# Laying out k by halves of its heads, reordering the first batch's denominators and splitting the last output tile

## The chip, the cores and the metric

One Trainium2 chip, of which the kernel uses one core. The figure compared is device microseconds (us) of one execution. The profile is a hardware recording of a single execution; its times are in us from the start of the span unless marked ns. In the text PE is TensorE (matrix products; PEld is its weight load), DVE is VectorE (elementwise), ACT is ScalarE (functions), POOL is GpSimd and SP is SyncE. The last two compute little here: POOL issues the transfers whose tables software writes, SP issues transfers through a hardware queue, and so does ACT at the start.

## The reference

```python
# q, k, v: 8 batches x 8 heads x 576 positions x 64, float32; pool = 8
k_p = k.reshape(B, H, Sp, pool, D).mean(axis=3)          # Sp = 72 pooled rows
v_p = v.reshape(B, H, Sp, pool, D).mean(axis=3)
scores = scale * np.matmul(q, k_p.transpose(0, 1, 3, 2))
scores = scores - np.max(scores, axis=-1, keepdims=True)
attn = np.exp(scores)
attn = attn / (np.sum(attn, axis=-1, keepdims=True) + 1e-09)
attn_out = np.matmul(attn, v_p)
x = attn_out.transpose(0, 2, 1, 3).reshape(B * S, H * D)  # 4608 tokens x 512
h = x @ w_in                                              # 512 -> 2048
g = 0.5 * h * (1.0 + np.tanh(c * (h + 0.044715 * h * h * h)))
out = g @ w_out                                           # 2048 -> 512, float32
```

## The kernel before

Attention runs batch by batch (8 of them), the two dense layers group by group: a group is 512 of the 4608 tokens, so there are 9 groups, g = 0 to 8. The attention output of a batch is written, transposed and in bfloat16, into `xT` (128 partitions = two heads x 64, four such pairs of heads, all tokens), which is what the first dense layer reads. The order of all instructions is written out by hand; each engine works through its own list in order.

**Loads.** Batch 0 comes in first: k and v by the SP and ACT queues, q by POOL (converted to bfloat16 on the way) in two halves of four heads. Then POOL loads the first dense weight `w_in` (two transfers), batch 1's k, q and v, the second dense weight `w_out` in four quarters, and q of batch 2. A k row is 8 positions x 64 = 512 floats, which are to be summed over the 8 positions. `load_k` (line 67) puts rows 0 to 511 of the 576 (8 heads x 72) on 128 partitions, four to a partition, and the 64 rows left over, all of them of head 7, in a fifth column on partitions 64 to 127. The same call loads v's pooled rows 64 to 71 of all heads (lines 74 to 76), 32 partitions for each four heads, into partitions 0 to 63 of that fifth column. `load_v` brings the other 64 rows per head.

**The first batch (lines 364 to 437).** DVE halves the 512 floats three times (`k_steps`: 512 to 256 to 128 to 64 sums, the last one written in bfloat16 to `kp`). PE transposes the result into a PSUM bank (`trans_k_mm`), and DVE copies it to `kT` twice, for each of the two halves of the columns of q (`trans_k_copy(b, e, ...)`, e = 0, 1). PE also transposes q (`trans_q`), copied out by ACT or DVE. `scores` multiplies and takes the exponential (ACT); `den0` sums the exponentials on PE against a tile of ones, `inverse0` takes logarithm and negative exponential on ACT, which gives 1/sum; `av0` multiplies by the pooled v, and `mult0` (DVE) scales the product into `xT`. c is the half of the tokens, pr the pair of heads. `spin` issues matmuls on a tile of zeros whose result nobody reads. After this come fills of constant regions for the later batches (lines 427 to 434) and the first eight matmuls of group 0.

**A group (lines 440 to 525).** First part: for each of 16 blocks of the 2048 hidden columns four matmuls of 128x512 (`p1_mm`, line 336), then the gelu on ACT (line 342). Beside it, DVE and PE prepare batch g + 1: `k_steps`, two small transfers that move v's last rows to their partitions (`v_moves`, SP queue), `v_steps`, and `trans_k` after block 9 (in group 0: q's transposes after blocks 12 to 15, `trans_k` after block 13 and `v_steps` at the end). Second part: for each of the four row tiles r of 128 tokens 16 matmuls (`p2_mm`, line 345) that accumulate in one bank, in which the score and value products of batch g + 1 are interleaved at fixed places (`pos`, line 501). In group 0 the first two row tiles advance together by quarters of `w_out` (line 516), so that the 9th, 17th and 25th matmuls are the first to read a new quarter. Groups 7 and 8 have no batch to interleave.

**Stores (lines 348 to 356).** When a row tile is complete, DVE copies it from PSUM to `osb` and four transfers of 32 tokens x 2 KB each go out on the SP queue; of the very last tile two go by ACT. The order of the tokens is such that each block of 32 columns of `xT` belongs to one (c, t): c is the half of the batch's tokens, t a block within it (0 to 8), and in the output a block's 32 rows are 18 rows apart. With `TP` = 9 blocks to a half,

```python
rows = out[b * S:(b + 1) * S].rearrange("(p t e) d -> e t p d", t=TP, e=2)
```

**Next loads.** In group g the loads for batch g + 2 are issued: q by POOL, then its transposition as one transfer on the SP queue (line 224), whose landing POOL waits for in `gate` (line 448), and then k and v by POOL.

Of the kernel before, what the change touches and what calls it, by code (L numbers as in the profile page):

```python
# [8 lines left out]
F32 = mybir.dt.float32  # L9
BF16 = mybir.dt.bfloat16  # L10
# [8 lines left out]
def kernel(  # L19
# [9 lines left out]
    nc = tc.nc  # L29
    B, H, S, D = q.shape  # L30
    Sp = S // 8
    N = B * S
    DM = H * D
# [9 lines left out]
    KR = 4  # L43
# [20 lines left out]

    kts = [consts.tile([128, KR + 1, 512], F32, name=f"kt{i}") for i in range(2)]

    def load_k(b, engs):
        rows = k[b].rearrange("h (j l) d -> (h j) (l d)", l=8)
        main = rows[0:128 * KR].rearrange("(p r) c -> p r c", r=KR)
        n = KR // len(engs)  # L70
        for i, eng in enumerate(engs):
            eng.dma_start(out=kts[b % 2][:, i * n:(i + 1) * n], in_=main[:, i * n:(i + 1) * n])
        engs[0].dma_start(out=kts[b % 2][64:128, KR], in_=rows[128 * KR:])
        rows = v[b].rearrange("h (j l) d -> j h (l d)", l=8)
        for i in range(2):
            engs[-1].dma_start(out=kts[b % 2][32 * i:32 * i + 32, KR], in_=rows[64:, 4 * i:4 * i + 4])

# [20 lines left out]
    load_k(0, [nc.sync, nc.scalar])  # L98
# [10 lines left out]
    load_k(1, [nc.gpsimd])  # L109
# [10 lines left out]
    kps = [consts.tile([128, KR + 2, D], BF16, name=f"kp{i}") for i in range(2)]  # L120
# [6 lines left out]
    nc.vector.memset(idle, 0.0)  # L127
    nc.vector.memset(kTs[0][0], 0.0)
# [9 lines left out]
    def add(o, a, b):  # L138
        nc.vector.tensor_tensor(out=o, in0=a, in1=b, op=ALU.add)  # L139

    def k_steps(b, c=slice(0, KR + 1)):


        t = kts[b % 2]
        return [lambda: add(t[:, c, 0:256], t[:, c, 0:256], t[:, c, 256:512]),
                lambda: add(t[:, c, 0:128], t[:, c, 0:128], t[:, c, 128:256]),
                lambda: add(kps[b % 2][:, c], t[:, c, 0:64], t[:, c, 64:128])]

    def v_moves(b):

        for i in range(2):
            nc.sync.dma_start(out=vps[b % 2][64 - 64 * i:72 - 64 * i, 4 * i:4 * i + 4, 0],
                              in_=kps[b % 2][32 * i:32 * i + 32, KR])
# [13 lines left out]
    def half_bank(bank):  # L167
        return PS[:, bank, :].bitcast(BF16)

    def trans_k_mm(b, bank, r0=0, r1=KR + 1, n=128):  # L170
        tp = half_bank(bank)[:, 0:(KR + 1) * 128].rearrange("p (r c) -> p r c", c=128)
        kf = kps[b % 2].rearrange("p r d -> p (r d)")
        for r in range(r0, r1):
            nc.tensor.transpose(out=tp[:n, r, :], in_=kf[:, r * D:r * D + n], identity=identb)  # L174

    def trans_k_copy(b, e, bank, lower=True, upper=True):


        tp = half_bank(bank)[0:D, 0:(KR + 1) * 128].rearrange("p (r c) -> p r c", c=128)
        o = kTs[b % 2][e][e * 64:(e + 1) * 64]  # L180
        copy = nc.vector.tensor_copy

        def heads(h0, h1, c0, j0, j1):
            copy(out=o[:, h0:h1, c0:c0 + (j1 - j0) * KR].rearrange("p h (j r) -> p h j r", r=KR),  # L184
                 in_=tp[:, 0:KR, h0 * KH:h1 * KH].rearrange("p r (h j) -> p h j r", j=KH)[:, :, j0:j1])

        if lower:
            heads(0, 4, 0, 0, KH)
        if upper:
            heads(4, H - 1, 64, 0, 16)  # L190
            heads(4, H - 1, 0, 16, KH)
            copy(out=o[:, H - 1, 64:72].rearrange("p (j r) -> p j r", r=KR),
                 in_=tp[:, 0:KR, (H - 1) * KH:128].rearrange("p r j -> p j r"))
            copy(out=o[:, H - 1, 72:128], in_=tp[:, KR, 64:120])
            copy(out=o[:, H - 1, 0:8], in_=tp[:, KR, 120:128])

    def trans_k(b, bank):
        trans_k_mm(b, bank)
        for e in range(2):
            trans_k_copy(b, e, bank)  # L200
# [17 lines left out]
    def trans_q(b, i, t0, n, bank, eng):  # L218
        trans_q_mm(b, i, t0, n, bank)
        trans_q_copy(b, i, t0, n, bank, eng)  # L220
# [107 lines left out]
    def o_bank(g, r):  # L328
        return 1 - x_bank(g) if r % 2 == 0 else x_bank(g)
# [14 lines left out]
    def p2_mm(g, r, fo):  # L344
        nc.tensor.matmul(out=PS[:, o_bank(g, r), :], lhsT=gTs[g][:, fo, r * 128:(r + 1) * 128], rhs=w_out_b[:, fo, :],  # L345
                         start=(fo == 0), stop=(fo == FO - 1))

    def store(g, r):
        osb = opool.tile([128, DM], F32, name="osb")
        nc.vector.tensor_copy(out=osb, in_=PS[:, o_bank(g, r), :])  # L350

        for n in range(4):
            b, c = divmod(g * GROUP + r * 128 + n * 32, S)
            rows = out[b * S:(b + 1) * S].rearrange("(p t e) d -> e t p d", t=TP, e=2)
            eng = nc.scalar if (g, r) == (NG - 1, 3) and n % 2 else nc.sync
            eng.dma_start(out=rows[c // CH, c % CH // 32], in_=osb[n * 32:(n + 1) * 32, :])


    def spin(n, bank):

        for _ in range(n):
            nc.tensor.matmul(out=PS[:, bank, :], lhsT=idle[:, 0:128], rhs=idle, start=True, stop=True)  # L362

    act_set(EXP_SET)
    spin(22, 1)
    for f in k_steps(0, slice(0, KR)):
        f()
# [5 lines left out]
    trans_k_mm(0, 4, 0, KR, D)  # L373
    trans_k_copy(0, 0, 4, upper=False)
    trans_q(0, *QG[0], 5, nc.scalar)
    trans_q(0, *QG[1], 6, nc.vector)
    trans_k_copy(0, 1, 4, upper=False)
# [3 lines left out]
    for f in k_steps(0, slice(KR, KR + 1)):  # L381
        f()
    scores(1, 0, 2)
    trans_k_mm(0, 4, KR, KR + 1, D)
    trans_k_copy(0, 0, 4, lower=False)

    for h in range(H):
        i = h // 4
        nc.tensor.matmul(out=PS[64 - 64 * i:72 - 64 * i, 7, h * D:(h + 1) * D],
                         lhsT=identb[0:64, 32 * i + h % 4:32 * i + 32:4], rhs=kps[0][0:64, KR],  # L390
                         start=True, stop=True)
# [9 lines left out]
    trans_k_copy(0, 1, 4, lower=False)  # L401
# [9 lines left out]
    spin(4, 4)  # L411
    av0(0, 0, 4)
    mult0(0, 0, 4)
    den0(0, 2, 2)
    inverse0(0, 2, 2)
    av0(1, 0, 0)
    mult0(1, 0, 0)
    spin(3, 6)
    den0(1, 2, 6)
    inverse0(1, 2, 6)  # L420
    spin(3, 4)
    av0(0, 2, 4)
    mult0(0, 2, 4)
    spin(3, 0)
    av0(1, 2, 0)
    mult0(1, 2, 0)
    for t in kps:
        nc.vector.memset(t[:, KR + 1], 0.0)
# [11 lines left out]
    for g in range(NG):  # L440
# [3 lines left out]
        def load_next():  # L444

            load_q(g + 2)
            trans_q_dma(g + 2)
            nc.gpsimd.tensor_copy(out=gate, in_=qTs[g + 2][0:1, 1, TP - 1, 0:2])  # L448
            load_k(g + 2, [nc.gpsimd])
            load_v(g + 2, [nc.gpsimd])  # L450
# [62 lines left out]
        seq = [(r, fo) for r in range(4) for fo in range(FO)]  # L513
# [3 lines left out]
        for m, (r, fo) in enumerate(seq):  # L517
            for f, a in todo.pop(m, []):
                f(*a)
            p2_mm(g, r, fo)  # L520
            if fo == FO - 1:
                store(g, r)
        for m in sorted(todo):
            for f, a in todo[m]:
                f(*a)

# [29 lines left out]
```

The softmax here doesn't subtract the row's maximum and nothing guards it: scores larger than these inputs give would overflow.

## Time and profile before

| what | value |
|---|---|
| runs | 309.18, 308.51, 309.1 us; median 309.1 |
| the profiled execution | 308.29 us, of which the recorded span is 306.5 |
| PE busy | 298.2 us (97%), 1518 matmuls |
| DVE, ACT, POOL busy | 150.4 (49%), 219.0 (71%), 36.3 (12%) |
| TensorE clock granted | 0.999 |
| first matmul of group 0 | 22.08 us |
| second part of group 0 begins | 37.18 us |
| last copy from PSUM (line 350) | 302.11, 0.69 us long |
| read from HBM, written to HBM | 36.70 MB, 9.44 MB |

"Busy" of PE is from modelled ends, so 97% says that PE nearly always has a matmul in hand, not that it runs at its peak. The chain of waits follows the work that ended last back to the start: its rows are a start, a length and what filled it, and a DMA in it is a transfer that something waited for. A row of the timeline is a start, a length, the engine, the line, the operation, and in brackets the idle time before it and what ended that.

### The profile page before, as it was taken

How to read it: one execution, taken by the hardware profiler on the slowest of the kernel's cores; microseconds unless marked ns; L12 is line 12 of the kernel's file. 1: busy time of each engine (PE TensorE's matmuls, PEld its weight loads, DVE VectorE, ACT ScalarE, POOL GpSimd, SP SyncE). 2: the span in 40 equal slices, each digit the busy share in tenths (PEclk: the TensorE clock that was granted, in tenths of full speed). 3: DMA queues.
4: the chain of work that ended last, by engine and by line, in shares of the span. 5: the costliest groups of instructions: out<-in, count | busy, mean ns of one | idle time of the engine just before them, and what ended most of it. 6: DMA issues, size and time to landing. Idle time of an engine off the chain costs nothing.

```text
span 306.5 us, 4325 instructions
## 1 busy us (share of the span) xinstructions
PE 298.2 (97%) x1518; PEld 157.4 (51%) x1548; DVE 150.4 (49%) x334; ACT 219.0 (71%) x402; POOL 36.3 (12%) x69
## 2 busy tenths in 40 slices
PE   8999999999999999999999999999999999999994
PEld 3555555555555555555555555555555555445441
DVE  5868557573677057806681559245933630110021
ACT  1686679868987798779977998789868987206400
POOL 7103002305004000220014000400000000000000
PEclk9999999999999999999999999999999999999999
DMA  7999996987957952596159725662101210121022
GB/s 225 266 257 253 214 186 137 299 176 177 269 146 167 247 122 51 114 282 156 34 112 266 168 56 106 200 151 71 35 1 36 63 41 2 34 70 34 2 70 68
DMA packets 30359, 41.12 MB, mean 134 GB/s; under 512 B 18113, under 2 KB 18113, under 8 KB 29441
## 3 DMA queue, kind: packets, MB, share of 16 engines
q0 software_dynamic: 7856, 25.43, 34.9%
q1 hardware_dynamic: 21888, 14.09, 19.2%
q10 hardware_dynamic: 592, 1.31, 1.2%
q8 instruction: 12, 0.20, 0.3%
q14 instruction: 11, 0.08, 0.1%
HBM read 36.70 MB, written 9.44 MB: 151 GB/s over the span
## 4 chain that ended last, share of the span: by engine, by line
PE 83%; DMA 12%; POOL 1%; issue 1%; ACT 0%; DVE 0%; POOLq 0%
PE PS L345 38%; PE PS L336 36%; DMA kt<-in_k_dram 7%; DMA w_out_b<-in_moe_w_out_dram 5%; PE PS L239 4%; PE PS L261 4%; PE PS L174 1%; POOL w_in_b L105 0%; POOL qb L86 0%; POOL w_out_b L113 0%; DVE osb L350 0%; ACT e L247 0%; ACT ld L269 0%; ACT ld L268 0%; POOL identb masks.py:199 0%
## 5 line engine op out<-in xcount | busy, mean ns | idle before, releaser
L345 PE MATMUL PS<-w_out_b,gT 128*128 128x512 bf16 x560 | 134.2, 379 | 0.9
L336 PE MATMUL PS<-xT,w_in_b 128*128 128x512 bf16 x563 | 126.2, 379 | 0.6
L342 ACT ACTIVATE gT<-PS 128x512 bf16<-128x512 f32 x144 | 81.1, 604 | 47.5 <-PE PS L336 47.4
L336 PEld LDWEIGHTS <-w_in_b 128*128 128x128 bf16 x576 | 64.7, 113 | 57.2
L345 PEld LDWEIGHTS <-gT 128*128 128x128 bf16 x576 | 56.1, 97 | 56.7 <-issue 1.1
L350 DVE COPY osb<-PS 128x512 f32<-128x512 f32 x36 | 24.9, 691 | 98.3 <-PE PS L345 95.3
L279 DVE TENSOR_TENSOR xT<-PS,rc 64x288 bf16<-64x288 f32 x112 | 51.0, 455 | 31.6 <-ACT rc L271 29.3
L247 ACT ACTIVATE e<-PS 72x576 bf16<-72x576 f32 (+1 forms) x64 | 41.0, 646 | 9.1 <-PE PS L239 8.2
L239 PE MATMUL PS<-qT,kT 128*72 128x288 bf16 (+1 forms) x128 | 25.9, 286 | 0.9 <-ACT qT L214 0.6
L271 ACT ACTIVATE rc<-ld 128x288 f32<-128x288 f32 x56 | 24.8, 443 | 1.8
L314 ACT ACT_TABLE_LOAD x17 | 21.8, 1283 | 4.3 <-issue 4.1
L268 ACT ACTIVATE ld<-PS 64x288 f32<-64x288 f32 x56 | 22.8, 407 | 1.3
L269 ACT ACTIVATE ld<-PS 64x288 f32<-64x288 f32 x56 | 22.5, 402 | 1.3
L261 PE MATMUL PS<-e,vp 72*128 72x288 bf16 (+1 forms) x112 | 23.1, 286 | 0.0
L139 DVE TENSOR_TENSOR kt<-kt 128x1280 f32<-128x1280 f32 (+5 forms) x18 | 18.8, 1044 | 5.5 <-DMA kt<-in_v_dram 2.6
L239 PEld LDWEIGHTS <-kT 128*72 128x72 bf16 (+1 forms) x128 | 13.2, 105 | 15.2 <-DVE qT L216 1.2
L448 POOL COPY gate<-qT 1x2 bf16<-1x2 bf16 x6 | 1.0, 174 | 140.0 <-DMA qT<-qb 140.0
L139 DVE TENSOR_TENSOR vt<-vt 128x1024 f32<-128x1024 f32 (+1 forms) x16 | 15.3, 956 | 1.8 <-DMA vt<-in_v_dram 1.5
L184 DVE COPY kT<-PS 64x288 bf16<-64x288 bf16 (+2 forms) x48 | 13.0, 319 | 6.2 <-PE PS L174 6.1
L362 PE MATMUL PS<-idle 128*128 128x512 bf16 x39 | 11.9, 447 | 1.2 <-DVE idle L127 1.2
L261 PEld LDWEIGHTS <-vp 72*128 72x128 bf16 (+1 forms) x112 | 11.0, 98 | 3.8
L81 POOL DMA_DIRECT2D vt<-in_v_dram x14 | 9.0, 655 | 7.5 <-DMA w_in_b<-in_moe_w_in_dram 5.5
(47 smaller groups left out, 90.0 us busy)
## 6 DMA issues: line engine op xcount, KB each, us to landing
out_dram<-osb SPq DMA_DIRECT2D x142, 64.0 KB
kt<-in_k_dram POOLq DMA_DIRECT2D x7, 1024.0 KB, 6.2
vt<-in_v_dram POOLq DMA_DIRECT2D x14, 512.0 KB, 8.6
qb<-in_q_dram POOLq DMA_DIRECT2D x7, 576.0 KB, 11.6
w_in_b<-in_moe_w_in_dram POOLq DMA_DIRECT2D x2, 1024.0 KB, 16.7
w_out_b<-in_moe_w_out_dram POOLq DMA_DIRECT2D x4, 512.0 KB, 13.9
kt<-in_k_dram POOLq DMA_DIRECT2D x7, 128.0 KB, 5.9
kt<-in_v_dram POOLq DMA_DIRECT2D x14, 64.0 KB, 5.7
```

The costliest lines, as they stand in the source:

```text
L139: nc.vector.tensor_tensor(out=o, in0=a, in1=b, op=ALU.add)
L239: nc.tensor.matmul(out=PS[:n, bank + e, :CH].rearrange("j (t p) -> j t p", p=32), lhsT=kTs[b % 2][c][:, h, :n], rhs=qTs[b][:, h // 4, :, h ...
L247: nc.scalar.activation(out=e[:n], in_=PS[:n, bank:bank + 2, :CH], func=ACT.Exp, scale=1.0 / 64.0)
L261: nc.tensor.matmul(out=PS[:, bank + x, :CH], lhsT=window(vps[b % 2][:n], 2 * pr + x), rhs=e[:n, x, :], start=True, stop=True)
L268: nc.scalar.activation(out=ld[0:64], in_=PS[64:128, bank, :CH], func=ACT.Ln)
L269: nc.scalar.activation(out=ld[64:128], in_=PS[0:64, bank + 1, :CH], func=ACT.Ln)
L271: nc.scalar.activation(out=rc, in_=ld, func=ACT.Exp, scale=-1.0)
L279: nc.vector.tensor_tensor(out=xT[rows, pr, col:col + CH], in0=PS[rows, bank + x, :CH], in1=rc[rows], op=ALU.mult)
L336: nc.tensor.matmul(out=PS[:, h_bank(g, fo), c0:c1], lhsT=w_in_b[fo // 8][:, ko, q * 512 + j:(q + 1) * 512:4], rhs=xT[:, ko, r0 + c0:r0 + c ...
L342: nc.scalar.activation(out=gTs[g][:, fo, :], in_=PS[:, h_bank(g, fo), :], func=ACT.Gelu_apprx_tanh)
L345: nc.tensor.matmul(out=PS[:, o_bank(g, r), :], lhsT=gTs[g][:, fo, r * 128:(r + 1) * 128], rhs=w_out_b[:, fo, :], start=(fo == 0), stop=(fo ...
L350: nc.vector.tensor_copy(out=osb, in_=PS[:, o_bank(g, r), :])
```

## The change

* k is loaded by halves of the heads. Half i (four heads, 288 rows) lies on 96 partitions, three rows to a partition: half 0 on partitions 0 to 95 in columns 0 to 2, half 1 on partitions 32 to 127 in columns 3 to 5. For batch 0 half 0 is loaded first, split between SP and ACT, then half 1, then v's last rows (now in partitions 0 to 31, columns 3 and 4).
* `k_steps` works on six columns, or on one half; transposes are six of 96 or 128 columns and of 64 wide weights; the copies to `kT` are one for half 0 and four for half 1.
* Regions that no load writes are filled with zeros: 32 partitions of one column before the loads, and at the end of the first batch partitions 96 to 127 of three columns in both buffers and 32 partitions of one column in the second.
* In the first batch both groups of q's first half are copied by ACT, k's transposes come after q's, the denominators of the later pairs come ahead of the outputs, and the number of spins falls from 40 to 27.
* A store issues one transfer for each run of blocks within a half (one or two for a row tile, all on SP) where it issued four.
* The last row tile is computed in two column parts, 384 and 128 wide, each copied and stored by itself.

```diff
-    KR = 4
+    KR = 3
...
+    def load_k(b, i, engs):
+        rows = k[b].rearrange("(i h) (j r l) d -> i (h j) (r l d)", i=2, r=KR, l=8)[i]
+        n = 4 * KH // len(engs)
+        for x, eng in enumerate(engs):
+            eng.dma_start(out=kts[b % 2][K0[i] + x * n:K0[i] + (x + 1) * n, KR * i:KR * i + KR],
+                          in_=rows[x * n:(x + 1) * n].rearrange("p (r c) -> p r c", r=KR))
+
+    def load_v_last(b, eng):
+        rows = v[b].rearrange("h (j l) d -> j h (l d)", l=8)
         for i in range(2):
-            engs[-1].dma_start(out=kts[b % 2][32 * i:32 * i + 32, KR], in_=rows[64:, 4 * i:4 * i + 4])
+            eng.dma_start(out=kts[b % 2][0:32, KR + i], in_=rows[64:, 4 * i:4 * i + 4])
...
-    load_k(0, [nc.sync, nc.scalar])
+    load_k(0, 0, [nc.sync, nc.scalar])
+    load_k(0, 1, [nc.sync, nc.scalar])
+    load_v_last(0, nc.scalar)
...
+    def load_k_all(b):
+        for i in range(2):
+            load_k(b, i, [nc.gpsimd])
+        load_v_last(b, nc.gpsimd)
...
+    nc.vector.memset(kts[0][0:32, 2 * KR - 1], 0.0)
...
+    def trans_k_mm(b, i, bank):
+        tp = half_bank(bank)[0:D, 0:2 * KR * 128].rearrange("p (r c) -> p r c", c=128)
+        n = K0[i] + 4 * KH
+        for r in range(i * KR, i * KR + KR):
+            nc.tensor.transpose(out=tp[:, r, 0:n], in_=kps[b % 2][0:n, r], identity=identb[0:n, 0:n])
...
+    def store(g, r, bank, c0=0, c1=DM):
+        if (g, r) not in osbs:
+            osbs[g, r] = opool.tile([128, DM], F32, name="osb")
+        osb = osbs[g, r]
+        nc.vector.tensor_copy(out=osb[:, c0:c1], in_=PS[:, bank, c0:c1])
 
-        for n in range(4):
-            b, c = divmod(g * GROUP + r * 128 + n * 32, S)
+        n = 0
+        while n < 4:
+            b, col = divmod(g * GROUP + r * 128 + n * 32, S)
+            c, t = col // CH, col % CH // 32
+            k = min(4 - n, TP - t)
             rows = out[b * S:(b + 1) * S].rearrange("(p t e) d -> e t p d", t=TP, e=2)
-            eng = nc.scalar if (g, r) == (NG - 1, 3) and n % 2 else nc.sync
-            eng.dma_start(out=rows[c // CH, c % CH // 32], in_=osb[n * 32:(n + 1) * 32, :])
+            nc.sync.dma_start(
+                out=rows[c, t:t + k, :, c0:c1], in_=osb[n * 32:(n + k) * 32, c0:c1])
+            n += k
...
-    spin(22, 1)
-    for f in k_steps(0, slice(0, KR)):
+    spin(13, 1)
+    for f in k_steps(0, 0, 1):
         f()
...
-    trans_k_mm(0, 4, 0, KR, D)
-    trans_k_copy(0, 0, 4, upper=False)
     trans_q(0, *QG[0], 5, nc.scalar)
-    trans_q(0, *QG[1], 6, nc.vector)
-    trans_k_copy(0, 1, 4, upper=False)
+    trans_q(0, *QG[1], 6, nc.scalar)
+    spin(3, 4)
+    trans_k_mm(0, 0, 4)
+    trans_k_copy(0, 0, 0, 4)
+    trans_k_copy(0, 1, 0, 4)
     scores(0, 0, 2)
     scores(0, 1, 0)
     spin(2, 7)
-    for f in k_steps(0, slice(KR, KR + 1)):
+    for f in k_steps(0, 1, 2):
         f()
     scores(1, 0, 2)
-    trans_k_mm(0, 4, KR, KR + 1, D)
-    trans_k_copy(0, 0, 4, lower=False)
+    trans_k_mm(0, 1, 4)
+    trans_k_copy(0, 0, 1, 4)
...
     inverse0(1, 0, 6)
-    spin(4, 4)
+    spin(2, 4)
+    den0(0, 2, 2)
+    inverse0(0, 2, 2)
+    spin(2, 4)
     av0(0, 0, 4)
     mult0(0, 0, 4)
-    den0(0, 2, 2)
-    inverse0(0, 2, 2)
+    den0(1, 2, 6)
+    inverse0(1, 2, 6)
     av0(1, 0, 0)
     mult0(1, 0, 0)
-    spin(3, 6)
-    den0(1, 2, 6)
-    inverse0(1, 2, 6)
-    spin(3, 4)
     av0(0, 2, 4)
     mult0(0, 2, 4)
-    spin(3, 0)
+    spin(2, 0)
     av0(1, 2, 0)
     mult0(1, 2, 0)
-    for t in kps:
-        nc.vector.memset(t[:, KR + 1], 0.0)
+    for t in kts:
+        nc.vector.memset(t[96:128, 0:KR], 0.0)
+    nc.vector.memset(kts[1][0:32, 2 * KR - 1], 0.0)
...
+        seq = [(r, fo) for r in range(4 if g + 1 < NG else 3) for fo in range(FO)]
...
+    for c0, c1, bank in ((0, 384, o_bank(g, 3)), (384, DM, 4)):
+        for fo in range(FO):
+            p2_mm(g, 3, fo, bank, c0, c1)
+        store(g, 3, bank, c0, c1)
```

## The prediction

> **What bounds the kernel now.** I read the page first, then the chain of waits, the timelines of the first 45 us and of the last 6, and last the DMA view of short windows.
>
> ```profile
> span 306.5 us, 4325 instructions
> PE 298.2 (97%) x1518; PEld 157.4 (51%) x1548; DVE 150.4 (49%) x334; ACT 219.0 (71%) x402; POOL 36.3 (12%) x69
> ```
>
> PE is the bound from group 0 on; only its two ends hold idle time. The chain of waits shows what releases it:
>
> ```profile
> 4.55 21.57 DMA kt<-in_k_dram
> 26.12 0.28 issue
> 26.40 0.86 POOL w_out_b L113 x2
> 27.46 16.53 DMA w_out_b<-in_moe_w_out_dram
> 44.03 0.81 PE PS L345 x3
> ...
> 300.19 1.91 PE PS L345 x8
> 302.11 0.69 DVE osb L350
> ```
>
> From 4.55 to 44.03 the chain is transfers, not PE: `w_out`'s last quarter lands at 27.46 + 16.53 = 43.99, and the 25th matmul of group 0's second part starts at 44.03. The completions in the trace put the four quarters at 36.6, 39.1, 41.6 and 44.0, one each 2.45 us, while PE needs 8 x 0.2155 + two to four 0.12 us products = 2.2 us for what uses one. The windows by 2 us show the transfer engines full from 4 to 44 us. So what the first batch gains is eaten here; what it loses costs only beyond PE's waits for quarters 2 to 4, about 0.1 + 0.2 + 0.2 = 0.5 us.
>
> The timeline of 8 to 15 us:
>
> ```profile
> 8.27 0.41 PE L174 MATMUL PS<-identb,kp 128*64 128x128 bf16 x4
> 8.59 0.75 POOL L86 DMA_DIRECT2D qb<-in_q_dram  x1 [1.77 <-DMA qb<-in_q_dram]
> 8.61 0.68 PE L204 MATMUL PS<-identb,qb 128*128 128x128 bf16 x9
> 9.85 0.65 PE L239 MATMUL PS<-qT,kT 128*72 128x288 bf16 x4 [0.56 <-ACT qT L214]
> 11.73 0.44 PE L239 MATMUL PS<-qT,kT 128*72 128x288 bf16 x2
> ```
>
> q's first half lands at 8.59: the second gate of the first batch, beside k's at 5.80. The end, from the timeline:
>
> ```profile
> 302.11 0.69 DVE L350 COPY osb<-PS 128x512 f32<-128x512 f32 x1 [2.76 <-PE PS L345]
> 302.84 0.85 ACTq L356 DMA_DIRECT2D out_dram<-osb  x2
> ```
>
> The last store's packets begin at 303.65, 0.81 us after issue, its last completion is at 305.20, and 1.29 us of closing steps follow to 306.49.
>
> **First batch.** The 576 KB of half 0 replace the 1 MB that landed at 5.80 and should land near 4.4, and DVE's three steps on 768, 384 and 192 elements (0.96 + 0.56 + 0.36 by the 1024, 512, 256 and 128 element rows 1.23, 0.69, 0.43, 0.29) end near 6.4 against 8.21. Nothing uses that: k's transposes now stand behind q's on PE (8.61). Nine q transposes (issue 9 x 0.057), three spins (0.2 each) and three k transposes end near 10.1; DVE's two copies of 0.45 each follow, and the scores start at 10.65 where they started at 9.85: 0.8 us late. ACT's second q copy (about 0.6 after 9.8) ends at 10.4, hidden. Half 1's steps are 1.9 us on DVE where the fifth column took 0.98, start behind the two copies at 11.05 and end at 13.0 (11.28 before). Behind them on PE stand three transposes, eight small products (0.29) and the fourth score pair (13.5 against 11.73), so ACT idles 0.8 us; behind them on DVE four copies, two casts of 0.42 and q's second half (0.9), so scores of the later pairs move from 14.04 to about 15.9. ACT then has four exponentials (2.6) and three inverses (1.35 each) without gaps: the inverse of (0, 2) ends near 21.7 (19.79 before), its product at 22.7, and group 0 starts near 22.9 instead of 22.08. The reorder saves ACT's gaps of 0.27 to 0.34; without it the start would be nearer 23.7. v's last rows go behind 64 KB more on ACT's queue and land near 10.4 (10.12), ahead of their use at 11.05.
>
> Then the fills: the trace has 0.485 us for 512 elements and 0.27 for 256, so 1536 elements are about 1.35; two of these, one of 512 and minus the old 0.13 are 3.1 us more on DVE before batch 1's `k_steps`, themselves 0.5 longer (six columns for five). These began at 28.40 and were done at 31.20, and DVE then waited 2.64 us for PE. Now they end near 35.3, just where PE wants `kp` (34.67 + 0.8); the copies behind end 0.9 late, v's sums at about 41.9 against 40.98, and the first value product (40.69) wants them: hidden to within 0.2 us because PE is itself 0.8 late. At the 25th matmul PE is near 44.5 instead of 44.03. I take **+0.5**, between 0 (half 1 of k lands and is reduced earlier than I think; below zero is excluded by the quarter at 43.99) and +1.3 (no cover).
>
> **Batches 1 to 7.** Six transposes for five. Five with 128 wide weights take 0.28 in the chain; four with 64 wide took 0.41 with a first of 0.23, so 0.06 each: six are 0.33 to 0.36. PE has nothing beside it: 7 x 0.06 = **+0.4**, between 0 (three of them move only 96 columns) and 0.6. DVE's 0.5 us per batch lies where it waits for PE or ACT. POOL issues four k transfers as before.
>
> **Stores.** SP issues 1 or 2 transfers per tile for 4, which frees SP; it was no bound. But their shape changes. In the trace's completions every 32-row store ends on sixteen transfer engines, and so do loads over 64 or 128 partitions; the load of v's last rows, whose DRAM side is 8 x 4 rows, ends on eight, and so do the moves of 8 partitions. The merged store's DRAM side is 4 x 32 rows (3 x 32 where a half ends), so by the nearest row it runs on **four** (three) engines, 32 packets of 2 KB one after another on each. A packet's price is in the DMA view, as share x 16 x window / packets that are not markers; alone (window 121.5 to 122.5) and queued (109 to 110):
>
> ```profile
> q1 hardware_dynamic: 96, 0.13, 55.2%
> ...
> q1 hardware_dynamic: 161, 0.22, 61.9%
> ```
>
> 64 packets at 16 x 0.552 / 64 = 0.138 us, and 108 at 16 x 0.619 / 108 = 0.092. Long queues on few engines are nearer the second, so a store takes 32 x 0.092 = 2.95 us, where four short ones took about 2.
>
> "DMA: Bandwidth & Descriptors" in the Trainium skill, section "Why a DMA increments its semaphore by 16 and not by 1", gives the rule: the largest number up to 16 that divides the slowest dimension of both sides. It speaks against the merged store, 4 against 128; by it and by the row alike the count is four. "SBUF — State Buffer", section on the DMA port swizzle, says partitions 32 apart share a port; the two engines of blocks 0 and 1 would then meet at one port, and the sum below would go by 0.138.
>
> **The end.** r = 0 to 2 of group 8 are issued near 292.5, 295.9 and 299.4 and start 0.8 later; at 2.95 each they end at 296.3, 299.9 and 303.2. The last tile's 16 matmuls of 384 columns take 2.6 us and those of 128 (0.058, the q transposes' spacing) 0.93, PE +0.1 in all. The copy of part one (0.56) ends at 301.85, its packets (0.069 each, 2.2 us) run behind r = 2 from 303.2 to 305.4; part two's copy (0.29) ends near 302.5 and its 32 packets of 512 B (0.023) follow to 306.1, completion +0.34: 306.45 against 305.20. **+1.25**, though PE and DVE are done 0.3 earlier. At 0.138 the queue backs up over all four tiles (297.7, 302.4, 306.8, 310.1, 311.2): +6.4. On sixteen engines: part two issued at 302.5, packets from 303.5 to 304.0, completion 304.35: -0.85.
>
> **Group 1.** Batch 2's v lands at 64.92, DVE waits for it, and its `kT` copies end at 69.9, 1.2 us before PE's use at 71.17. Four merged stores now sit on engines that carry these loads, 3 us of packets more on them from 51 to 63; I expect v 1.2 late, covered, and `k_steps` late by 0.3: **+0.2**, between 0 and 1.5. Later batches have over 10 us to spare.
>
> Sum: 0.5 + 0.4 + 1.25 + 0.2 = 2.35 us. The profiled execution took 308.29 (span 306.5 and 1.8 around it), 0.8 under the median 309.1; the sum on the median is **311.4**.
>
> **Rivals.** (1) Two engines block each other in the merged stores: +6.4 at the end, up to +1.5 in group 1, 309.1 + 0.5 + 0.4 + 6.4 + 0.7 = 317. For it: the 0.138 of short stores. Against: 0.092 once they queue. (2) The merged store still spreads over sixteen engines, for which the sixteen completions of every store now speak and the eight of v's last rows speak against: 309.1 + 0.5 + 0.4 - 0.85 = 309.15, not slower; with the first batch free, 308.4. It decides at eight engines: there the last store ends about where it does now. (3) PE's clock: PE idles from the 13th spin (6.2) to 8.6. The spins ran at 0.427 us each until 5.78 and 0.204 after; fallen back for 3 us, the first batch would lose some 1.5 us more: 312.9. No idle time of PE over 1.2 us before the end shows whether it falls.
>
> **How the numbers follow.** A measurement of this kernel tells about 0.2% (0.6 us) from no change. Four engines near the short packet price, 310 to 313.5: 0.50. Rival 1, in whole or in part, above 313.5: 0.25. Rival 3: 0.08, on the slower side too. Rival 2: 0.17, of which 0.07 lies within 0.2% and 0.10 is faster (the first batch and the transposes at their lower ends). Slower 0.83, same 0.07, faster 0.10. The range leaves out what lies below 309.5 (about 0.1) and the last of rival 1: 309.5 to 317.2.
>
> **What would show it.** Right: completions of 4 or 3 to a store; DMA busy for some 2 us longer after the last copy; closing steps after 307.5; group 0 starting at 22.5 to 23.3 and the 25th matmul between 44.0 and 44.8; 0.33 to 0.36 for six transposes. Wrong: stores with sixteen completions; `w_out`'s last quarter landing before 43.5, which would turn the first batch into a gain or loss of its own; a stall of PE in group 1 at the k transposes.

## The result and the profile after

| | before | changed |
|---|---|---|
| median of 4 runs, us | 308.96 (308.51 to 309.18) | 323.57 (319.8 to 324.8) |
| ratio | 1 | 1.0434, 95% interval 1.0345 to 1.0523 |
| profiled execution, of which the span | 308.29, 306.5 | 323.62, 321.8 |

The change costs 14.6 us where 2.35 were forecast; the time lies above the stated range (309.5 to 317.2). The ratios leave out every run more than 1.5% above the fastest of its kernel: 324.8 here, and below 312.31 in e8 and two executions, of 458 us (e5) and 396 us (e8), that ran at a granted clock of 0.66 and 0.75 from end to end, so that these two kernels were profiled a second time (e10, e11).

From the page of the changed kernel: the span, the busy time of the engines, and the granted clock of TensorE in 40 slices of 8 us.

```profile
span 321.8 us, 4245 instructions
...
PE 305.5 (95%) x1559; PEld 160.1 (50%) x1559; DVE 156.7 (49%) x320; ACT 219.6 (68%) x403; POOL 36.1 (11%) x69
...
PEclk9559999997999999999999999999999999999996
```

Before, PE had 298.2 us of work and every slice of the clock read 9. Now slices 2 and 3 (8 to 24 us) read 5 and slice 10 (72 to 80 us) reads 7. Most of the 7.3 us by which PE's busy time grew is not new work but the same work at a slower clock. Laying the starts of the groups in the two traces side by side, and the last matmul's end, places the 15.36 us by which the span grew:

| stretch | before, us | after, us | growth |
|---|---|---|---|
| start to group 0 | 22.08 | 28.40 | 6.32 |
| group 0 (to group 1's start at 55.62, 62.59) | 33.54 | 34.19 | 0.65 |
| group 1, first part | 14.09 | 17.95 | 3.86 |
| first parts of groups 2 to 6, each | 14.09 | 14.35 | 0.26 x 5 = 1.30 |
| end of the last matmul to the end of the span | 4.41 | 7.60 | 3.19 |

All other parts agree within 0.04 us. **The first batch.** The timeline of PE, 4 to 12 us:

```profile
3.73 2.77 PE L385 MATMUL PS<-idle 128*128 128x512 bf16 x7
10.53 1.14 PE L219 MATMUL PS<-identb,qb 128*128 128x128 bf16 x9 [4.03 <-DMA qb<-in_q_dram]
11.46 1.06 PE L385 MATMUL PS<-idle 128*128 128x512 bf16 x2
```

q's first half lands at 10.48 (by the completions; 8.30 before, where PE began on it at 8.61), PE stands idle for 4.03 us ahead of it, and nine transposes then take 1.14 us instead of 0.68. The windows of four us (not counting the brackets, the seventh number is the granted clock) show how long that lasts; the trace's record of the clock has the fall at 9.35 and the rise at 23.00:

```profile
4.00:8.00 4.00, 2.50 (x7) 0.74 (x5) 1.86 (x3) 1.28 (x1) 2.74 (x5) 1.00 1.04 217
8.00:12.00 4.00, 1.47 (x11) 1.20 (x12) 0.00 (x0) 0.72 (x2) 0.76 (x1) 0.67 1.08 288
12.00:16.00 4.00, 3.46 (x14) 1.51 (x12) 2.50 (x5) 1.65 (x3) 0.66 (x1) 0.50 1.12 256
16.00:20.00 4.00, 4.00 (x30) 2.61 (x29) 2.36 (x9) 2.47 (x4) 0.62 (x1) 0.50 1.12 211
20.00:24.00 4.00, 3.94 (x17) 2.12 (x16) 3.65 (x9) 2.05 (x5) 0.00 (x0) 0.62 1.11 248
```

**Group 1.** The chain of waits has a transfer in it that was not there before; its rows are a start, a length and what filled it:

```profile
58.05 11.66 DMA kt<-in_v_dram
...
69.83 1.77 DVE kt L151
71.60 0.02 issue
71.62 0.97 DVE kt L151
...
73.23 0.48 PE PS L188 x6
```

v's last rows of batch 2 land at 69.71 (60.52 before), DVE's sums begin there, and PE, which wants `kp` for the transposes, idles 1.85 us and then takes 6.89 us from the first of the next 24 matmuls to the second part (5.18 before), at a lowered clock again (0.5 from 74.20 to 77.61). Before, the same sums and `kp` were done at 63.52, and PE came to the transposes at 64.25, with 0.7 us to spare:

```profile
60.64 2.35 DVE L139 TENSOR_TENSOR kt<-kt 128x1280 f32<-128x1280 f32 x2 [2.62 <-DMA kt<-in_v_dram]
63.03 0.49 DVE L139 TENSOR_TENSOR kp<-kt 128x320 bf16<-128x320 f32 x1
```

**The end**, from the timeline of the last 22 us:

```profile
304.60 10.55 SPq L377 DMA_DIRECT2D out_dram<-osb  x6
...
314.28 0.29 DVE L369 COPY osb<-PS 128x128 f32<-128x128 f32 x1 [0.34 <-PE PS L360]
```

DVE is done at 314.57. A merged store of four blocks has completions from four transfer engines, one of three blocks from three, and a block on its own from sixteen. The last ones of r = 0, 1, 2 come at 310.44, 314.02 (its three merged blocks at 313.84) and 317.5, those of the two column parts at 320.0 and 320.75, and 1.1 us of closing steps follow.

### The profile page after: what moved, and what is told of

Its sections match the earlier page's. It is cut to its first block, busy times and chain, and to the rows that moved or that the text cites. A ratio compares the mean times of both kernels' runs of the same rounds, so it can differ in the third digit from the quotient of the medians.

```text
span 321.8 us, 4245 instructions
## 1 busy us (share of the span) xinstructions
PE 305.5 (95%) x1559; PEld 160.1 (50%) x1559; DVE 156.7 (49%) x320; ACT 219.6 (68%) x403; POOL 36.1 (11%) x69
## 3 DMA queue, kind: packets, MB, share of 16 engines
q10 hardware_dynamic: 480, 1.25, 1.4%
## 4 chain that ended last, share of the span: by engine, by line
PE 75%; DMA 11%; issue 8%; POOL 2%; DVE 1%; POOLq 0%; DVEq 0%
PE PS L360 34%; PE PS L351 32%; DMA kt<-in_k_dram 7%; PE PS L276 4%; PE PS L254 4%; DMA kt<-in_v_dram 4%; DVE kt L151 1%; PE PS L188 1%; POOL qb L89 1%; POOL kt L73 0%; POOL w_in_b L110 0%; POOL w_out_b L123 0%; DVE kp L151 0%; POOL kt L79 0%; DVE osb L369 0%
## 5 line engine op out<-in xcount | busy, mean ns | idle before, releaser
L360 PE MATMUL PS<-w_out_b,gT 128*128 128x512 bf16 (+2 forms) x592 | 136.2, 373 | 0.0
L351 PE MATMUL PS<-xT,w_in_b 128*128 128x512 bf16 x576 | 129.1, 383 | 0.0
L360 PEld LDWEIGHTS <-gT 128*128 128x128 bf16 x592 | 57.1, 98 | 55.6 <-issue 0.4
L369 DVE COPY osb<-PS 128x512 f32<-128x512 f32 (+2 forms) x37 | 25.1, 678 | 99.5 <-PE PS L360 99.2
L254 PE MATMUL PS<-qT,kT 128*72 128x288 bf16 (+1 forms) x128 | 27.4, 302 | 0.5 <-DVE kT L199 0.5
L151 DVE TENSOR_TENSOR kt<-kt 128x768 f32<-128x768 f32 (+4 forms) x18 | 22.0, 1220 | 7.2 <-DMA kt<-in_v_dram 4.8
L254 PEld LDWEIGHTS <-kT 128*72 128x72 bf16 (+1 forms) x128 | 14.0, 111 | 15.3 <-issue 0.8
L199 DVE COPY kT<-PS 64x252 bf16<-64x252 bf16 (+4 forms) x80 | 16.3, 266 | 10.0 <-PE PS L188 9.8
L385 PE MATMUL PS<-idle 128*128 128x512 bf16 x27 | 11.1, 559 | 1.5 <-DVE idle L137 1.2
## 6 DMA issues: line engine op xcount, KB each, us to landing
vt<-in_v_dram POOLq DMA_DIRECT2D x14, 512.0 KB, 10.1
```

What stands on the lines that cost most here:

```text
L254: nc.tensor.matmul(out=PS[:n, bank + e, :CH].rearrange("j (t p) -> j t p", p=32), lhsT=kTs[b % 2][c][:, h, :n], rhs=qTs[b][:, h // 4, :, h ...
L351: nc.tensor.matmul(out=PS[:, h_bank(g, fo), c0:c1], lhsT=w_in_b[fo // 8][:, ko, q * 512 + j:(q + 1) * 512:4], rhs=xT[:, ko, r0 + c0:r0 + c ...
L360: nc.tensor.matmul(out=PS[:, bank, c0:c1], lhsT=gTs[g][:, fo, r * 128:(r + 1) * 128], rhs=w_out_b[:, fo, c0:c1], start=(fo == 0), stop=(fo ...
L369: nc.vector.tensor_copy(out=osb[:, c0:c1], in_=PS[:, bank, c0:c1])
```

## The experiments

Theory at the start: the first batch pays for q's late landing twice, once in waiting and once in clock; the merged stores pay in group 1 and at the end. The rivals name another part for each piece.

**Four transfers to a store, the rest as changed (e1).**

```diff
-            k = min(4 - n, TP - t)
+            k = 1
```

> The changed kernel with four transfers of 32 rows per row tile again (all on SP), everything else as changed. Theory A (the merged stores on four engines hold up batch 2's loads and the end): the first part of group 1 shrinks from 17.9 us to 14.5 to 15.5, and from the last matmul to the end it is 3.7 to 4.2 us instead of 7.6, so about 317 us. Theory B (the k loads on 96 partitions hold up group 1, stores only the end): group 1 stays at 17 to 18 us, about 320 us. The first batch is the same in both, group 0 from 28.4 us.

Measured: 315.53 us (315.18, 315.88), ratio 1.0234 (1.0189 to 1.0278). The first part of group 1 is 14.35 us again, and 5.26 us follow the last matmul. So in this kernel the merged stores cost 3.6 us in group 1 and 2.3 at the end, and theory A's place for the larger part is right. The 5.26 us are more than its 3.7 to 4.2, which e6 takes up. Group 0 starts at 25.89, earlier than in the changed kernel and than both theories had it, though nothing at the head differs:

```profile
10.34 1.14 PE L219 MATMUL PS<-identb,qb 128*128 128x128 bf16 x9 [3.44 <-DMA qb<-in_q_dram]
```

PE idles 3.44 us here and the clock falls too, but is back at about 17 us (its mean from 16 to 20 is 0.88) where the changed kernel's is back at about 23.

**36 spins at the start (e2).**

```diff
-    spin(13, 1)
+    spin(36, 1)
```

> The changed kernel with 36 spins for 13 at the start, which keep PE at work until q's first half lands near 10.6. Theory A (half of the first batch's delay is the clock that falls while PE idles 4 us): the spins and products between 10.6 and 23 us run at 0.21 instead of 0.43 us per 512 columns, group 0 starts near 25 to 26 instead of 28.4, and the time is 2.5 us lower, about 321. Theory B (only the transfers and the order count): group 0 starts within 0.7 us of 28.4.

Measured: 324.68 us (323.98, 325.38), ratio 1.053 (1.0466 to 1.0595). The head is as theory A has it: no fall of the clock, although 36 spins were too many, since q landed at 9.82 and the transposes stood behind them until 11.72; from there to group 0 (25.75) it is 14.03 us. But theory A's 321 us are not reached and nothing is gained, for group 1's first part takes 21.51 us instead of 17.95:

```profile
74.56 0.77 PE L188 MATMUL PS<-identb,kp 96*64 96x96 bf16 x6 [5.25 <-DVE kp L151]
```

PE comes to group 1 at 60.52 instead of 62.59, and v's rows of batch 2 don't come earlier. What the head gains, that wait takes back. The two faults cover each other, so each had to be tried without the other.

**k's old layout, the rest as changed (e3).** The edit puts back `load_k`, `k_steps`, `trans_k_mm`, `trans_k_copy` and the fills of the kernel before, under the new order, the 13 spins, the merged stores and the column parts:

```diff
-    load_k(0, 0, [nc.sync, nc.scalar])
-    load_k(0, 1, [nc.sync, nc.scalar])
-    load_v_last(0, nc.scalar)
+    load_k(0, [nc.sync, nc.scalar])
...
-    trans_k_mm(0, 0, 4)
-    trans_k_copy(0, 0, 0, 4)
-    trans_k_copy(0, 1, 0, 4)
+    trans_k_mm(0, 4, 0, KR, D)
+    trans_k_copy(0, 0, 4, upper=False)
+    trans_k_copy(0, 1, 4, upper=False)
```

> The changed kernel with k laid out, loaded, summed and transposed as before; order, spins, merged stores and column parts stay. Theory A (96 partitions make the k loads slow): q's first half lands at 8.6 instead of 10.7, the quarters of w_out at 36.6 to 44.0 instead of 40.5 to 47.9, six transposes are five again (14.1 instead of 14.35 us for the first part of groups 2 to 6), group 0 starts between 22.9 (the forecast) and 25 (if the clock still falls in 2.4 us of idle PE). What group 1 and the end lose stays: 309 + 1 to 3 + 2 to 4 + 3.2, about 315 to 318. Theory B (the order of the first batch is what costs): group 0 starts at 26 or later with q at 8.6.

Measured: 319.77 us (319.68, 319.86), ratio 1.0371 (1.0335 to 1.0407). q lands at 8.43, PE idles 1.81 us and keeps its clock, and group 0 starts at 21.68, 0.4 earlier than before the change. So in a run that keeps its clock the order of the first batch costs nothing at group 0's start, and the lateness there belongs to k's layout. The time lies above theory A's 315 to 318, because group 1's first part takes 20.93 us, 6.8 more than before where 2 to 4 were allowed.

**The transfers alone (e4).** 

> No attention and no dense layers: only transfers, each alone, of the shapes in dispute; the output is left at zeros. If the number of partitions decides, 96 partitions of 6 KB take 0.40 us a packet (2.4 us for six on each of sixteen engines) and 64 partitions the same, while 128 of 6 KB take 0.235 (1.9 us for eight) and 128 of 8 KB 0.31; if the packet's size or the queue decides, 6 KB takes the same with 96 and 128 partitions. A merged store of 4 x 32 rows of 2 KB ends on four engines 4.5 to 5.5 us after its issue, four single ones 2.5 to 3 us after the first issue, each on sixteen; if two of the four engines get into each other's way, the packets take 0.14 and more, if not, 0.084.

First to last packet, from the trace's packets (by SP and by POOL, 64 partitions: 1.75 and 2.09 us for 384 KB; 128 partitions with 8 KB to each, 1 MB, as in k's old main part: 3.41 and 3.47):

| load, 6 KB to a partition | by SP, us | by POOL, us |
|---|---|---|
| 128 partitions, 768 KB | 3.03 | 3.02 |
| 96 partitions from 0, 576 KB | 2.80 | 2.97 |
| 96 partitions from 32, 576 KB | 2.99 | 2.87 |
| 48 + 48 by SP and ACT | 3.02 | |

A quarter fewer bytes than 768 KB take nearly the same time (up to 8% less), by either queue, and 44% fewer than 1 MB take 11 to 18% less; each load was timed once. Neither expectation holds as written: a packet of 6 KB takes 0.24 to 0.37 us (medians) on 96 partitions, 0.23 on 128 and 0.30 to 0.34 on 64. The Trainium skill, "SBUF — State Buffer", section "The DMA setup-cost knee", has the rule that a transfer-bound load should use 128 partitions; these rows agree with it. Why 96 are no faster is not settled here: by the port map in the same page's section "Door 1: The DMA port swizzle" the fullest port serves eight partitions with 64, 96 and 128 alike, so that 64 would be as slow too, and they are not.

DVE waits for each store by writing to the source again, so its rows give issue to completion (issues at 70.19, 76.3, 79.6 and 85.8):

```profile
76.23 0.06 DVE L71 MEMSET buf<- 128x1 f32 x1 [5.88 <-DMA out_dram<-buf]
79.51 0.06 DVE L71 MEMSET buf<- 128x1 f32 x1 [3.22 <-DMA out_dram<-buf]
85.75 0.06 DVE L71 MEMSET buf<- 128x1 f32 x1 [6.17 <-DMA out_dram<-buf]
91.11 0.06 DVE L71 MEMSET buf<- 128x1 f32 x1 [5.30 <-DMA out_dram<-buf]
```

One merged store of four blocks takes about 6.0 us, the same bytes in four transfers 3.2, each more than expected; three blocks take 6.2 and two 5.3, so the count of bytes hardly matters: the completions come from four, three and two engines, which leaves each with 32 packets whatever the number of blocks. The packets of the store of four run from 71.48, 1.29 us after its issue, to 75.78, 84 ns each (median), but the first 1.4 us hold only a few, of up to 0.92 us. 128 contiguous rows of 2 KB went out on sixteen engines in 2.15 us.

**Merged stores alone on the kernel before (e5, profiled again as e10).**

```diff
-        for n in range(4):
-            b, c = divmod(g * GROUP + r * 128 + n * 32, S)
+        n = 0
+        while n < 4:
+            b, col = divmod(g * GROUP + r * 128 + n * 32, S)
+            c, t = col // CH, col % CH // 32
+            k = min(4 - n, TP - t)
...
-            eng = nc.scalar if (g, r) == (NG - 1, 3) and n % 2 else nc.sync
-            eng.dma_start(out=rows[c // CH, c % CH // 32], in_=osb[n * 32:(n + 1) * 32, :])
+            nc.sync.dma_start(
+                out=rows[c, t:t + k, :], in_=osb[n * 32:(n + k) * 32])
+            n += k
```

> The kernel before with one change: a row tile's four stores are merged into one or two transfers, all on SP (the last tile stays whole). Theory A (the merged stores by themselves hold up batch 2's loads and end late): the first part of group 1 grows from 14.1 to 18 to 21 us, the time after the last matmul from 4.4 to 7 to 8 us, stores complete on 4 or 3 engines, total 316 to 319. Rival B (the loads were late only because k's new layout had already made them late; before, they had 1.2 us to spare): group 1 grows by 1 to 2 us, the end by 2.5, total 312 to 313.

> The kernel before with merged stores alone, once more for its profile. Theory A: the first part of group 1 takes 20 to 22 us for 14.1, because the merged stores of group 0 hold up batch 2's loads; groups 2 to 7 as before; 7 to 8 us after the last matmul; total 318 to 320. Rival B: group 1 as before, and 1 us or more in each later group.

Measured: 318.48, 319.55 and 319.82 us, ratio 1.0326 (1.0285 to 1.0367); the second profile took 320.27. Its first part of group 1 takes 22.53 us (theory A had 20 to 22), and 7.72 follow the last matmul; every other part is as before. Rival B of e5 is out: the stores need no help from the layout. The waits between 55 and 75 us (engine, line, what for: us in total, times, longest) and the timeline of PE:

```profile
DVE kt L139 <- DMA kt<-in_v_dram: 8.8, 1, 8.8
...
PE PS L174 <- DVE kp L139: 5.3, 1, 5.3
```

```profile
69.96 0.72 PE L174 MATMUL PS<-identb,kp 128*128 128x128 bf16 x5 [5.30 <-DVE kp L139]
70.47 5.71 PE L336 MATMUL PS<-xT,w_in_b 128*128 128x512 bf16 x13
```

The completions of v's last rows, issued at 54.12 (53.92 before), tell why. Before, the sixteen engines finish between 59.05 and 60.52. With merged stores, nine finish between 60.52 and 62.2, two by 63.51, and the last five between 64.87 and 66.91, some 4 us after the rest. In the changed kernel the split is cleaner: twelve by 66.01, four between 68.33 and 69.71. DVE's sums start only after the last of the sixteen (67.03 in e10). That the late ones are those that carry the stores is inferred from their number (stores end on four), as the completions don't name their engine.

**Merged stores from group 1 on (e9).**

```diff
-            k = min(4 - n, TP - t)
+            k = min(4 - n, TP - t) if g else 1
```

> The kernel before with merged stores, but those of group 0 left as four transfers each. Merged stores in all groups cost 10 us in the kernel before. Theory A (the merged stores of group 0 meet batch 2's loads, and those of group 8 end late; all others are hidden): the first part of group 1 takes 14.1 us as before, and only the end is longer, 7 to 8 us after the last matmul for 4.4: total 312 to 313. Rival B (later groups stall too, or the stall moves to group 2, where the stores of group 1 meet batch 3's loads): 315 or more.

Measured: 312.81 us (312.27 to 313.8), ratio 1.013 (1.0107 to 1.0154). Group 1's first part is 14.09 us and PE waits for nothing there:

```profile
65.34 0.44 PE L174 MATMUL PS<-identb,kp 128*128 128x128 bf16 x5
```

No later group takes longer than before; 7.49 us follow the last matmul. Group 1 starts at 56.71 (55.62 before), as `w_out`'s last quarter lands at 45.09 in this profile, though the head is that of the kernel before. Theory A holds in both places: it is group 0's stores that meet batch 2's loads, and the end costs 3.1 us more.

**Column parts alone on the kernel before (e6).**

```diff
-        seq = [(r, fo) for r in range(4) for fo in range(FO)]
+        seq = [(r, fo) for r in range(4 if g + 1 < NG else 3) for fo in range(FO)]
...
+            k = 1
...
+    for c0, c1, bank in ((0, 384, o_bank(g, 3)), (384, DM, 4)):
+        for fo in range(FO):
+            p2_mm(g, 3, fo, bank, c0, c1)
+        store(g, 3, bank, c0, c1)
```

> The kernel before with one change: the last row tile is computed, copied and stored in two column parts, 384 and 128 wide, each with four transfers, all eight on SP. Theory A (SP's issues, one after the other, set the end, as the 5.3 us after the last matmul with the same stores suggest against 4.4 before): the end comes 0.6 to 1.0 us later, total 309.6 to 310. Rival B (the smaller last copy lets the stores go earlier): 0.3 us earlier, total 308.6. The groups ahead of it stay as before.

Measured: 310.01 us (12 runs), before 309.62 (23 runs on the same chip); ratio 1.0018 (0.9999 to 1.0036). 5.34 us follow the last matmul: theory A's size, though the whole is hardly told from no change. The completions of the eight transfers come 0.45 us apart, one after another, from 304.05 to 307.14: eight issues on one queue set the end, not PE or the bytes.

**The layout with its clock kept (e7):** e1 with 28 spins.

```diff
-    spin(13, 1)
+    spin(28, 1)
...
-            k = min(4 - n, TP - t)
+            k = 1
```

> The changed kernel with four transfers to a store and 28 spins at the start where it has 13, so that PE idles less than 1 us before q's first half lands near 10.3. Both theories: granted clock 1.00 throughout the first 24 us, group 0 starts 14.0 us after q's transposes, near 24.2 (25.9 with 13 spins and these stores). Theory A (k on 96 partitions has also pushed w_out's last quarter from 44.0 to 48, and that sets the start of group 1): group 1 starts at 59.5 to 59.8 where it started at 60.1, total 314.9 to 315.3; PE waits for w_out by 1 us or more in the second part of group 0. Rival B (w_out keeps up): group 1 at 58.4, total 313.8.

Measured: 314.38 us (313.54 to 314.59), ratio 1.0158 (1.0119 to 1.0197). The clock is 1.00 in every window; group 0 starts at 23.99, 14.04 us after q's transposes, and group 1 at 59.48. From the timeline of PE:

```profile
9.95 0.68 PE L219 MATMUL PS<-identb,qb 128*128 128x128 bf16 x9 [0.85 <-DMA qb<-in_q_dram]
...
37.51 0.48 PE L188 MATMUL PS<-identb,kp 96*64 96x96 bf16 x6 [0.76 <-DVE kp L151]
...
42.59 1.46 PE L360 MATMUL PS<-w_out_b,gT 128*128 128x512 bf16 x6 [0.28 <-DMA w_out_b<-in_moe_w_out_dram]
...
45.67 1.02 PE L360 MATMUL PS<-w_out_b,gT 128*128 128x512 bf16 x4 [0.70 <-DMA w_out_b<-in_moe_w_out_dram]
```

Group 0's second part, to group 1's start, takes 19.3 us where e1 had 18.0. `w_out`'s last quarter lands at 47.50 (43.99 before), and with the clock kept it is this that holds PE: theory A's start of group 1, to 0.1 us. The time lies 0.5 us under A's and 0.6 over B's; the trace decides it. What the fall of the clock costs when the stores are apart is known only roughly: the ratios of e1 and e7 differ by 0.0076, or 2.3 us, but their intervals overlap, and in the two profiles group 1 starts at 60.08 and 59.48, 0.6 us apart: of the 1.9 us between their starts of group 0 (25.89 and 23.99), e7's longer second part, with its waits for `w_out`, takes back 1.3.

**Order and column parts alone (e8, profiled again as e11),** k's old layout as in e3, four transfers to a store, and

```diff
-            nc.sync.dma_start(
+            eng = nc.scalar if (g, r) == (NG - 1, 3) and n % 2 else nc.sync
+            eng.dma_start(
```

> The changed kernel with k's old layout and its fills, four transfers to a store, and in the last tile every second transfer on ACT; left of the change are the order of the first batch, its fewer spins and the column parts. Theory A (the order costs nothing, group 0 starting near 21.7 as it did with k's old layout and merged stores, and the last tile gains about 0.3 us): total 308.0 to 309.0, the same as before within 0.2%. Rival B (the 1.2 us by which group 0 was longer there belongs to the order): group 1 starts near 56.7 where it started at 55.6, total 309.9 to 310.5.

> The same kernel as in the run on the order and the end, for its profile and a narrower interval. Theory A: group 0 starts at 21.7, group 1 between 55.3 and 56, some 4.1 us from the last matmul to the end for 4.4; total 308.0 to 309.0, ratio 0.996 to 1.000. Rival B: group 1 starts near 56.7, total 309.9 or more.

Measured: 308.41 us (median of eleven, 307.6 to 312.31), ratio 0.9987 (0.996 to 1.0014); again 308.26 (12 runs, 307.78 to 310.66), ratio 0.9993 (0.9974 to 1.0013). Theory A by the medians; but the profiled run was one of the three above 310, with group 0 at 25.13, not 21.7 (of the other two, 310.66 has a granted clock of 0.983 like this one, 310.27 one of 0.998, so that its lateness is something else):

```profile
8.34 0.68 PE L204 MATMUL PS<-identb,qb 128*128 128x128 bf16 x9 [1.92 <-DMA qb<-in_q_dram]
```

```profile
8.00:12.00 4.00, 3.11 (x20) 1.82 (x21) 1.54 (x4) 1.34 (x3) 1.39 (x2) 0.65 1.09 296
12.00:16.00 4.00, 4.00 (x26) 2.25 (x24) 2.02 (x9) 2.52 (x5) 0.02 (x1) 0.50 1.12 227
16.00:20.00 4.00, 4.00 (x22) 2.45 (x21) 3.47 (x10) 2.32 (x4) 0.62 (x1) 0.57 1.12 211
```

An idle time of 1.92 us lost the clock here, and one of 1.81 us in e3 did not. The traces' record of the granted clock bears on why so little decides. In all these runs it changes only at the ends of windows of 3.41 us, which begin at another time in each run. In the window ahead of the fall PE was busy for 1.49 us here (5.79 to 9.20), for 0.57 in the changed kernel (5.93 to 9.35) and for 0.15 in e1 (6.74 to 10.15), and for 1.56 ahead of the fall in the changed kernel's group 1 (70.79 to 74.20). In e3's window around the same idle time it was 1.60 (6.26 to 9.67), and the clock stayed. So in these runs the border lies at a little under half a window of work, and where the window falls differs from run to run.

**The same with 21 spins (e12).**

```diff
-    spin(13, 1)
+    spin(21, 1)
```

> The kernel of the order and the end (k's old layout, four transfers to a store, last tile over SP and ACT) with 21 spins at the start where it has 13, so that PE is busy until q's first half lands near 8.4. In the last profile of it PE idled 1.92 us there and then ran at a granted clock of 0.5 until 18 us; in an earlier one with the same head it idled 1.81 us and kept 1.00. Theory A (the idle time decides over the clock, by chance near its limit): every run has the clock, group 0 starts at 21.6, the runs lie between 307.3 and 308.6 with none near 310.7, median 307.9, ratio 0.994 to 0.998. Rival B (the fall has another cause): runs of 310 or more still occur, and the median stays at 308.3 to 308.6.

```profile
8.57 0.68 PE L204 MATMUL PS<-identb,qb 128*128 128x128 bf16 x9 [0.85 <-DMA qb<-in_q_dram]
```

Measured: 308.23 us, before 309.04 on the same chip; ratio 0.9972 (0.9958 to 0.9987). All twelve runs lie between 307.74 and 308.67, against 307.6 to 312.31 with 13 spins: theory A, its median 0.3 us too low. This kernel is a little faster than the one before. 3.87 us follow its last matmul (4.41 before), with the eight completions some 0.2 us apart over two queues. Group 0 starts at 21.77, but its lead is lost at `w_out`, whose last quarter lands at 44.77 in this profile; group 1 starts at 56.40 (55.62 before). That is no cost of the order: in e9, with the old order, it starts at 56.71 when that quarter lands at 45.09.

## Why the prediction was wrong

The sign, the price of a packet and the number of engines held; every term of the sum was too small. The sign was not right for its reasons: the two largest losses, 6.97 and 3.86 us, stood in the sum as 0.5 and 0.2.

* **First batch, +0.5, measured +6.97 at group 1's start.** The step that failed is the first: "The 576 KB of half 0 ... should land near 4.4". It let the bytes set the time, and e4 shows that they don't (2.80 to 3.02 us for 576 KB, 3.41 and 3.47 for 1 MB). The halves landed at 5.73 and 8.40, where the old main part was there at 5.80, and q's first half, left at 8.59 in the sum, landed at 10.48. Of the 6.32 us at group 0's start, 1.92 are the later transposes of q (10.53 for 8.61). The chain from there to group 0 was rightly worked out: 22.9 - 8.6 = 14.3 forecast, 14.04 measured with the clock kept, 13.47 before. The other 17.87 - 14.04 = 3.83 us (17.87 from 10.53 to 28.40) are the clock, by the comparison with e7. That was rival 3, at a chance of 0.08 and +1.5 us: its idle time was taken from a landing that moved, and with it from 2.4 us to 4.03. The statement that a gain was excluded by `w_out`'s quarter at 43.99 took that landing as fixed as well; it moved to 47.9.
* **Fills, "hidden to within 0.2 us".** PE waits 0.77 us for `kp` at 41.91, and group 0's first part grows by 1.09. DVE went from its last product to batch 1's sums in 9.16 us where it took 5.29: 3.9 more, not 3.1. Most of what was missed is the idle 0.38 and 0.27 us ahead of the two large fills.
* **Transposes, 0.06 a batch, measured 0.26.** Six take 0.41 us in the chain where five took 0.28, and the 24 matmuls behind them 5.30 instead of 5.18. 0.33 to 0.36 was taken for the six, and nothing for what follows them.
* **Group 1, +0.2 (0 to 1.5), measured +3.86 (0.26 of it the transposes), and 8.4 in e10.** The step "3 us of packets more on them ...; I expect v 1.2 late" was mis-sized: v's rows came 6.4 us late in e10. It treated a delay on four engines almost as one shared by sixteen. Its reading of what was to spare, 1.2 us at the `kT` copies, also passed over the nearer limit: `kp` had 0.7 us before PE's transposes. In the changed kernel half of this is covered, as PE comes to group 1 6.7 us later than in e10 (62.59 for 55.86) and v's rows only 2.8 (69.71 for 66.91).
* **The end, +1.25, measured +3.19.** Four engines and 0.092 us a packet (84 ns measured) were right. What the trace of before had no row for is the slow start of each merged store, 1.4 us in e4, which makes 4.3 us of a store where 2.95 were counted, and its first packet 1.29 us after the issue where 0.8 was. So each merged store of the last group takes 5.8 to 6.1 us from issue to completion, as it does alone in e4 (6.0), and the last part is issued only at 314.62. Rivals 1 and 2 are out: neither 0.138 us a packet nor sixteen engines. That PE and DVE finish earlier for the column parts was worth nothing on one queue.
* **The order.** Costed at a gain of 0.8 us (22.9 for 23.7), it gave 0.3 to 0.4 with k's old layout where the clock stayed: 21.68 and 21.77 for 22.08.

The pieces on their own come to more than the whole: 10.1 us for merged stores (0.0326 x 309) and 7.2 for all the rest with the stores apart (e1, 0.0234 x 309), 17.3 against 14.6. They overlap: the later PE comes to group 1, the less it waits for batch 2's loads.

Open: why 96 partitions are no faster than 128; why the low clock lasts two windows in one run (e1) and four in another (the changed kernel) with the same head; and why `w_out`'s last quarter lands anywhere from 43.7 to 45.4 with k's old layout (43.72 in e11, 44.77 in e12, 45.36 in e3). The order need not be the cause, since it is 43.99, 44.23 (e10) and 45.09 (e9) with the old order.

## What to carry to other kernels

Work out a transfer by its slowest engine, not by its bytes: one that uses four engines can hold up whatever needs all sixteen, and one on 96 partitions may cost what 128 do. When a landing gates the start, treat the landings after it as moved too, and see what PE does in the gap: here the fall of the clock cost twice the delay that brought it on (3.83 us for 1.92). When two faults lie one behind the other, take each away alone and both together, since the later one hides the repair of the earlier.

## What the runs showed that was not expected

* PE's clock fell to a half after idle times of 1.92, 3.44 and 4.03 us (and 1.85 to 5.3 in group 1), not after 0.85 or 1.81; it then stayed there for one to four windows of 3.41 us: 13.65 us in the changed kernel's head, 10.24 in e11's, 6.83 in e1's, and 3.41 or 6.83 in group 1. In group 1 one window full of work brought it back, in the heads of the changed kernel and of e11 it took two. "TensorE: Matmul & The Clock Gate" in the Trainium skill, section "What's actually happening", gives a free-running window of about 3.4 us, with a fall after an idle window and a rise after a busy one. The windows agree with it. That the window ahead of the fall has to be idle doesn't fit (PE was busy for 1.49 of 3.41 us in e11), nor that one full window always suffices for the rise; here the measurement decides.
* A merged store of two blocks (128 KB) takes 5.3 us from issue to completion, one of four 6.0, and four single ones 3.2.
* Transfers of 16 and 48 KB in a row on one queue complete 0.45 us apart (e6), and 0.2 us apart over two queues (e12).
